# Strassen's scheme for the last group's up projections, and memory visits by 64x64 tiles, in a fused attention and expert kernel

## Chip, cores and metric

One core of a Trainium2 chip runs the whole program in one launch. The metric is the device time in microseconds (us) of an execution, lower is better, given as the median of several runs. Engines are called PE (TensorE's matmuls), PEld (its weight loads), DVE (VectorE), ACT (ScalarE), POOL (GpSimd) and SP (SyncE, which issues the DMAs).

## What is computed

```python
# attention: q, k, v are (4, 8, 576, 64) in float32
a = softmax(causal(q @ k.T / 8)); local = a @ v
q_p = phi(q)                                   # elu + 1
mem = (q_p @ M_prev) / (q_p @ z_prev + 1e-6)   # 64x64 memory of each head
x = sigmoid(beta) * mem + (1 - sigmoid(beta)) * local     # 2304 tokens x 512
# expert: w_gate, w_val 512 x 1536, w_out 1536 x 512
out = (sigmoid(x @ w_gate) * (x @ w_val)) @ w_out
```

The weights arrive as float64 bits and are converted on the chip.

## The kernel before

**Groups.** The 2304 tokens are cut into six groups of 384. Group 0 and group 5 hold the tails of the batches (192 tokens of each of two batches), groups 1 to 4 the first 384 tokens of one batch each. The expert of a group runs while the attention of later groups is done beside it, and the last group's expert has no attention left beside it.

**Expert (`moe`).** Twelve passes, one for each block of 128 of the 1536 inner columns. Every operand is held as a high and a low part in float32r, and a product is three matmuls: high by high, high by low, low by high. A pass has an up part, gate and value projection with 24 matmuls that load a 128x128 block of weights and move 384 tokens (2 projections x 4 blocks of 128 inner features x 3), and a down part of the pass before it (`down`) with 9 matmuls that load 128 tokens and move 512 columns. Between the two stands the gate chain: tanh of the gate's bank on ACT (L895), times the value's bank on DVE (L897), a high copy `gh` on ACT, the rest `gl` on DVE. Each matmul of the program has its own weight load, also where the same block is loaded twice running. The expert's matmuls all have line L313. The up parts take banks 3 and 4 ("gv"), the down parts add up in banks 0 to 2.

**Weights.** In group 0 DVE and ACT convert them (L805 to L816). The gate's high and low parts stay in `wg`; the value's and the output's go to DRAM (`scratch`) and come back by DMA through a ring of three buffers `sv` in the groups that follow.

**Attention.** It goes by pairs of heads: `scores` (`heads`, L561), softmax on DVE and ACT (L623, L635), `turn` (transposes), `values` (L317), `across` (into the group's tokens `xh`, `xl`). The 16 pairs of groups 1 to 4 have two items of scores each. Behind the scores of their first item (256 keys) come the memory visits (`terms`, L518): both heads lie on a half of the array's rows each, three blocks of 128 queries are loaded as 64x128 blocks, and 65 columns move. In the pairs of groups 0 and 5 the visits and the scores ahead of them are by 64x64 blocks already. Float32 matmuls stand twice in the trace for each one in the code.

**Order.** Nothing is issued as the code runs: `Program` collects every instruction with a cost and its dependencies, a list scheduler with priorities (`LEAD`, by part and engine) puts them in an order for each engine, a random search of 800 rounds betters the priorities, and the order is then fixed. An engine works its list in that order.

Of the kernel before, what the change touches and what calls it, by code (L numbers as in the profile page):

```python
# [9 lines left out]
F32 = mybir.dt.float32  # L10
F32R = mybir.dt.float32r
# [10 lines left out]
VC = 66  # L22
# [13 lines left out]

WORLDS = (380.0, 0.85, 0.0), (400.0, 0.85, 0.03), (350.0, 1.0, 0.06)

LEAD = {("attention", "pe"): 150, ("weights", "sp"): 200, ("first", "sp"): 1000, ("second", "sp"): 98}

WAKE = {
    "act": {"act": 0.14, "dve": 0.13, "pe": 0.26, "pool": 0.2, "sp": 0.14},
# [196 lines left out]
def tile_attention_memory_moe(  # L239
# [26 lines left out]
    class Ring:  # L266
# [10 lines left out]
        def take(self):  # L277
            i = self.at % self.n
            self.at += 1
            k = pg.renew((self.name, i))  # L280
            if i not in self.tiles:
                home = self.tags.get(i)
                if home:

                    hosts, ring, at = home
# [4 lines left out]
                    pg.before[(self.name, i)] = set(pg.touched[(ring, at)][1]) | pg.before[(self.name, i)]  # L290
                    pg.closed.add((ring, at))
# [8 lines left out]
    turns = {"att": 0, "gv": 0, "second": 0}  # L300

    def bank(kind):
        ids = {"att": att_banks, "gv": [3, 4], "second": [0, 1]}[kind]
# [7 lines left out]
    def matmul(out, lhsT, rhs, n, r, w, start, stop):  # L311
        pe(0.004 + max(n, 128) / 2250.0,
           lambda: nc.tensor.matmul(out=out, lhsT=lhsT, rhs=rhs, start=start, stop=stop), r, w)  # L313

    def product(out, lhsT, rhs, n, r, w, start, stop):
        pe(0.068 if n <= 100 else 4 * n / 2385.0,
# [8 lines left out]
    def copy(out, in_, n, r, w):  # L325
        act(n, lambda: nc.scalar.copy(out=out, in_=in_), r, w)  # L326
# [76 lines left out]
    kq_r = Ring("kq", [128, 2 * GT], F32R, 4, {i: (in_wt, "wt", i) for i in range(4)})  # L403
    ql_r = Ring("ql", [128, GT], F32R, 2, {i: (in_wr, "wr", 2) for i in range(2)}, init=half)
# [4 lines left out]
    tl_r = Ring("tl", [128, 2 * DM], U16, 2, {i: (turned, "wr", 1) for i in range(2)})  # L409
    xs_r = Ring("xs", [128, 3, 2, D], F32, 2)  # L410
    xm_r = Ring("xm", [128, 3, 2, D], F32, 2)
    rs_r = Ring("rs", [128, 3, 2], F32, 2)
# [96 lines left out]
    def terms(u, sp, js, at):  # L509

        for c in range(3):
            cells = [(0, 128 * c, 0, 128)]
            if u.tail:
                es = (0, 1) if c == 2 else (c, c)
                cells = [(e, e * TL + (128 if c == 2 else m0), m0, m0 + 64) for e, m0 in zip(es, (0, 64))]
            for e, q, m0, m1 in cells:
                for j, r in enumerate(js):
                    nc.tensor.matmul(  # L518
                        out=sp[j][0][m0:m1, at + MC * c:at + MC * c + MC], lhsT=u.ph[r, q:q + m1 - m0],
                        rhs=mem[u.g][e][0][r, u.p, MC * j:MC * j + MC], start=True, stop=True)  # L520
# [44 lines left out]
    def scores(n, x):  # L565
# [11 lines left out]

        def part(i, cells):
            sp = [bank("att") for _ in js]
            more = pair and i == 1 or not u.tail and x == 0  # L580
            work, at = [], 0
            for y, k0, k1 in cells:
                c, q0, W = u.items[x][y]
                if pair:
                    es = [(0, 128, 0, 64), (1, 128, 64, 128)]
                    mk, mk_k = (mask2[:, :k1 - k0], "mask2") if i else (mask[:, :k1 - k0], "mask")
                else:
                    es = [(c if u.tail else 0, q0, 0, 128)]
                    mk, mk_k = mask[:, 512 - W:], "mask"
                work.append((y, es, k0, k1, at, mk, mk_k))  # L590
                at += k1 - k0
            if more:
                u.told = [(sp[j][0][:, at:at + 3 * MC].rearrange("p (c j x) -> p c j x", c=3, j=1),
                           sp[j][1], j, j + 1) for j in range(2)]

            def together():
                for _, es, k0, k1, o, _, _ in work:
                    heads(u, es, sp, js, k0, k1, o)
                if more:
                    terms(u, sp, js, at)  # L600
# [217 lines left out]
    def weights(F):  # L818
# [5 lines left out]
        if g and at < sv_r.n:  # L824
            ready_w[F] = ready_w[F - 2 * at - 1]
            return
        part, pg.part = pg.part, "weights"
        sv_r.at = at if g % 2 == 0 else sv_r.n - 1 - at % sv_r.n
        sv, k = sv_r.take()
        kg = [("wg", f, "h"), ("wg", f, "l")]  # L830
        if g == 0:
# [14 lines left out]
    def rows(g, t):  # L846
# [4 lines left out]
            return [((b + t) * S + GT, 0, 128)]  # L851
        return [((b + e) * S + GT + 128, 64 * e, 64) for e in range(2)]

    def moe(g):
        (xh, _), (xl, _), xk = x_t[g]
        prev = None
# [4 lines left out]
        def down(f, gh, gl, wo):  # L861
# [3 lines left out]
            for t in order:  # L865
# [5 lines left out]
                           f == 0 and i == 0, f == NF - 1 and i == 2)  # L871
                yield

        for f in range(NF):
            cur = ready_w[g * NF + f]
            pz = [bank("second" if g == 0 and f == 1 else "gv") for _ in range(2)]
            turns = [(part, kd) for part in range(2) for kd in range(KD)]
            if f == 0 or g == 0 and f == 1:
# [28 lines left out]
                kept[NF - 1 - f]([gh[1]])  # L907
            if prev:
                yield from down(*prev)
            weights(g * NF + f + 2)  # L910
            prev = (f, gh, gl, cur[2])
        yield from down(*prev)
        for t in order:
            acc, acc_k = accs[t]
            ob, ob_k = (ob_r if g < NG - 1 else at_r).take()
# [110 lines left out]
```

## Time and profile before

| what | value |
|---|---|
| median of 3 runs | 629.06 us (628.87 to 629.29) |
| profiled execution | 629.38 us |
| its span, first to last instruction | 627.5 us |
| PE busy / PEld busy | 610.7 / 535.5 us |
| DVE / ACT busy | 409.8 / 267.5 us |
| mean granted clock of TensorE | 0.995 |

A matmul's row in the timeline gives its start and its duration to the end of its results, so durations overlap; what a matmul costs in a stream is the distance from its start to the next one's, here called its step. An "x12" row is twelve instructions merged. Times in timelines and chains are from the span's start.

### The profile page before, as it was taken

The numbers are of one execution on the slowest core, as the hardware profiler recorded it, in microseconds if no ns is written. First come the engines' busy times: TensorE is split into PE (matmuls) and PEld (weight loads), VectorE is DVE, ScalarE is ACT, GpSimd is POOL, SyncE is SP. The second block draws the span as 40 slices with busy tenths as digits, with TensorE's granted clock in tenths as the row PEclk, the third lists the DMA queues.
The fourth block names the chain that finished last, engine by engine and source line by source line (L and its number), as shares of the span: only waits on it lengthen the run. The fifth ranks groups of instructions, "written<-read, shape, count | busy, mean of one in ns | idle before, by whom it ended". The sixth has DMA issues, their size and how long they took to land.

```text
span 627.5 us, 12396 instructions
## 1 busy us (share of the span) xinstructions
PE 610.7 (97%) x4928; PEld 535.5 (85%) x4928; DVE 409.8 (65%) x1091; ACT 267.5 (43%) x536; POOL 9.5 (2%) x51
## 2 busy tenths in 40 slices
PE   6889999998999999999999999999999999999996
PEld 3559888986898988898988898988898989999995
DVE  4999999998865568756566756678697573121211
ACT  6997667756533324333242434246363221211111
POOL 2000000000000000000000000000000000000000
PEclk9999999999999999999999999999999999999999
DMA  8667878796499699668786467978668994225351
GB/s 303 231 229 240 270 283 276 249 311 225 93 281 297 210 217 254 116 174 216 187 219 209 107 173 211 223 203 229 139 147 219 181 218 146 100 84 191 146 194 57
DMA packets 103130, 126.42 MB, mean 201 GB/s; under 512 B 79648, under 2 KB 81696, under 8 KB 95776
## 3 DMA queue, kind: packets, MB, share of 16 engines
q1 hardware_dynamic: 102928, 125.36, 69.7%
q8 instruction: 39, 0.64, 0.4%
q10 hardware_dynamic: 144, 0.26, 0.1%
q14 instruction: 19, 0.16, 0.1%
HBM read 89.43 MB, written 17.30 MB: 170 GB/s over the span
## 4 chain that ended last, share of the span: by engine, by line
PE 90%; DVE 6%; DMA 1%; ACT 1%; issue 1%; DVEq 0%; ACTq 0%
PE bank L313 72%; PE bank L317 7%; PE bank L561 6%; PE bank L320 2%; PE bank L518 2%; DVE a L623 1%; DMA wr<-in_w_dram 1%; DVE wt L809 1%; DVE wt L812 1%; ACT a L635 1%; DVE sv L336 1%; DMA kp<-in_qk_dram 1%; DVE wt L807 0%; DVE ph L492 0%; ACT wt L805 0%
## 5 line engine op out<-in xcount | busy, mean ns | idle before, releaser
L313 PE MATMUL bank<-xh,wg 128*128 128x384 f32 x576 | 163.4, 341 | 2.2 <-ACT wg L326 2.0
L313 PE MATMUL bank<-xh,sv 128*128 128x384 f32 x576 | 164.1, 341 | 0.3 <-DVE th L897 0.2
L313 PE MATMUL bank<-sv,gh 128*128 128x512 f32 x432 | 136.2, 396 | 0.3 <-ACT gh L326 0.3
L313 PEld LDWEIGHTS bank<-xh,wg 128*128 128x128 f32 x576 | 104.8, 188 | 8.8 <-ACT wg L326 2.8
L313 PEld LDWEIGHTS bank<-xh,sv 128*128 128x128 f32 x576 | 104.8, 188 | 2.8 <-DVE sv L336 0.7
L897 DVE SCALAR_TENSOR_TENSOR th<-th,bank 128x384 f32<-128x384 f32 x72 | 39.7, 551 | 98.0 <-PE bank L313 96.9
L313 PE MATMUL bank<-xl,wg 128*128 128x384 f32 x288 | 97.8, 340 | 0.0
L313 PE MATMUL bank<-xl,sv 128*128 128x384 f32 x288 | 97.6, 339 | 0.0
L313 PEld LDWEIGHTS bank<-sv,gh 128*128 128x128 f32 x432 | 79.5, 188 | 14.2 <-ACT gh L326 0.7
L895 ACT ACTIVATE th<-bank 128x384 f32<-128x384 f32 x72 | 35.3, 490 | 131.0 <-PE bank L313 130.8
L635 ACT ACTIVATE a<-a,st 128x256 f32<-128x256 f32 (+4 forms) x144 | 77.3, 581 | 26.9 <-DVE st L623 26.3
L623 DVE CUSTOM_DVE_ANT_0 a<-bank,mask 128x256 f32<-128x256 f32 (+3 forms) x144 | 64.9, 485 | 36.3 <-PE bank L561 18.3
L313 PE MATMUL bank<-sv,gl 128*128 128x512 f32 x216 | 84.8, 396 | 0.0
L326 ACT CAST gh<-th 128x384 fp32r<-128x384 f32 x72 | 36.9, 513 | 104.7 <-DVE th L897 104.5
L313 PEld LDWEIGHTS bank<-xl,wg 128*128 128x128 f32 x288 | 54.1, 188 | 4.1 <-issue 1.0
L561 PE MATMUL bank<-kp 64*128 64x256 f32 (+4 forms) x352 | 52.5, 452 | 4.0 <-DMA kp<-in_qk_dram 4.0
L653 DVE COPY at<-tl_wr 128x1024 uint16<-128x1024 uint16 (+1 forms) x72 | 46.8, 654 | 12.7 <-DMA tl_wr<-pl_wr 12.5
L313 PEld LDWEIGHTS bank<-xl,sv 128*128 128x128 f32 x288 | 54.1, 188 | 0.5
L336 DVE TENSOR_TENSOR gl<-th,gh 128x384 fp32r<-128x384 f32 x72 | 39.8, 554 | 15.5 <-ACT gh L326 15.2
L313 PEld LDWEIGHTS bank<-sv,gl 128*128 128x128 f32 x216 | 40.5, 188 | 9.4 <-DVE gl L336 0.4
L649 DVE COPY pl_wr<-a 128x1024 uint16<-128x1024 uint16 (+1 forms) x72 | 41.8, 593 | 3.8 <-ACT a L635 3.8
L561 PEld LDWEIGHTS bank<-kp 64*128 64x128 f32 (+1 forms) x352 | 23.1, 169 | 23.8 <-issue 10.5
(66 smaller groups left out, 588.0 us busy)
## 6 DMA issues: line engine op xcount, KB each, us to landing
sv<-w SPq DMA_DIRECT2D x45, 1024.0 KB, 5.4
wr<-in_w_dram SPq DMA_DIRECT2D x36, 512.0 KB, 4.6
kp<-in_qk_dram SPq DMA_DIRECT2D x32, 384.0 KB, 4.1
w<-sv SPq DMA_DIRECT2D x12, 1024.0 KB, 6.6
out_dram<-ob SPq DMA_DIRECT2D x14, 256.0 KB, 2.2
vt<-in_vp_dram SPq DMA_DIRECT2D x8, 330.0 KB, 4.8
vr<-in_vp_dram SPq DMA_DIRECT2D x8, 330.0 KB, 4.1
mb<-in_mz_dram SPq DMA_DIRECT2D x8, 260.0 KB, 3.5
```

Of the source, the lines that this page charges most:

```text
L313: lambda: nc.tensor.matmul(out=out, lhsT=lhsT, rhs=rhs, start=start, stop=stop), r, w)
L317: lambda: nc.tensor.matmul(out=out, lhsT=lhsT, rhs=rhs, start=start, stop=stop), r, w)
L320: pe(0.110, lambda: nc.tensor.transpose(out=out, in_=in_, identity=identity), r, w)
L326: act(n, lambda: nc.scalar.copy(out=out, in_=in_), r, w)
L336: dve(n, lambda: nc.vector.tensor_tensor(out=out, in0=in0, in1=in1, op=op), r, w)
L561: nc.tensor.matmul(out=sp[j][0][m0:m1, at:at + k1 - k0], lhsT=kp[r, u.qa + q:u.qa + q + m1 - m0], rhs=kp[r, u.ka + k0:u.ka + k1], start=Tr ...
L623: dve(m + 60, lambda aj=aj, sj=sj, pj=pj, o=o, m=m, mk=mk, b=b0 + k0: nc.vector.tensor_tensor_reduce(out=aj[:, b:b + m], in0=pj[:, o:o + m ...
L635: act(W + 120, lambda aj=aj, sj=sj, b=b0, W=W: nc.scalar.activation(out=aj[:, b:b + W], in_=aj[:, b:b + W], func=AF.Exp, scale=-1.0, bias= ...
L649: dve(2 * W, lambda: nc.vector.tensor_copy(out=pl.rearrange("p (two w) -> p two w", two=2), in_=src), r, [pk], fast=True)
L653: dve(2 * W, lambda: nc.vector.tensor_copy(out=dst, in_=tl.rearrange("p (two w) -> p two w", two=2)), [lk], [key], fast=True)
L895: act(GT, lambda: nc.scalar.activation(out=th, in_=pg_[:, :GT], func=AF.Tanh, scale=0.5), [pg_k], [th_k])
L897: dve(GT, lambda: nc.vector.scalar_tensor_tensor(out=th, in0=th, scalar=1.0, in1=pv[:, :GT], op0=ALU.add, op1=ALU.mult,), [th_k, pv_k], [t ...
```

## The change

Two things. **First**, `terms` and the scores ahead of it load two blocks of 64x64 for each block of 64x128, in the 16 pairs of groups 1 to 4. **Second**, in the last group gate and value projection of a pass are seen as one product of a 2x2 block matrix of weights (gate and value by halves of the 512 input features) with a 2x2 block matrix of tokens (halves of the features by halves of the 384 tokens), done by seven block products in place of eight (`seven`): each has 2 feature blocks x 3 matmuls that load 128x128 and move 192 tokens, so 42 matmuls of 192 tokens stand for 24 of 384. Its inputs are sums: four of the tokens for the whole group (`token_sums`), four of the weights for each pass (`weight_sums`: eight adds or subtractions of 256 columns on DVE, and four splits into high and low, each a copy on ACT and a subtraction on DVE). For passes over blocks 8, 5, 3 and 1 the weight sums are made in groups 2 and 3 and written to DRAM (`save`); for the other eight in or ahead of the last group. Results are put together on DVE from the banks (five adds of 192 columns, the value's product in two halves). Buffers of the attention are given new tenants, and two more sets of value and output weights are held in the last group. The planner's priority of the sums is lower by 60, and its cost of a block of scores with a visit rises from 0.63 to 0.8 us beside the keys' share.

```diff
+SAVED = (8, 5, 3, 1)
+LEAD = {..., ("sums", "dve"): -60, ("sums", "act"): -60}
...
+        ids = {"att": att_banks, "gv": [3, 4], "second": [0, 1], "last": [3, 4, 5, 6, 7]}[kind]
...
+    un_r = Ring("un", [128, DM], F32R, 16, ...)     # weight sums, in a, vr, vt, kp, mb
+    xv_r, xo_r = ...                                # two more sets of weights, in at
...
     def terms(u, sp, js, at):
         for c in range(3):
-            cells = [(0, 128 * c, 0, 128)]
+            cells = [(0, 128 * c + m0, m0, m0 + 64) for m0 in (0, 64)]
...
                     es = [(c if u.tail else 0, q0, 0, 128)]
+                    if more:
+                        es = [(0, q0, 0, 64), (0, q0 + 64, 64, 128)]
...
-                    pe(4 * at / 2385.0 + (0.63 if more else 0.3), together,
+                    pe(4 * at / 2385.0 + (0.8 if more else 0.3), together,
...
+    def weight_sums(F, raws, made):
...
+        whole(a, g, 0)
+        whole(b, v, 0)
+        over(c, b, a)
+        done(2, c)
+        whole(c, g, 1)
+        over(a, a, c, plus)
+        done(0, a)
+        over(b, a, b)
+        done(1, b)
+        whole(c, v, 1)
+        over(c, c, b)
+        done(3, c)
...
+    def seven(g, F, t):
...
+        x, y, z = (bank("last") for _ in range(3))
+        def times(out, a, b, first):
+            (o, ok), (ah, al, ahk, alk), (bh, bl, bhk, blk) = out, a, b
+            for d in range(2):
+                at = slice(d * 128, d * 128 + 128)
+                for i, (l, lk, r, rk) in enumerate(((ah, ahk, bh, bhk), (ah, ahk, bl, blk), (al, alk, bh, bhk))):
+                    matmul(o[:, :HT], l[:, at], r[:, d], HT, lk + rk, [ok], first and d == 0 and i == 0, d == 1 and i == 2, not first)
...
+        times(x, a11, b11, True)
+        copy(p1, x[0][:, :HT], HT, [x[1]], [p1k])
+        times(y, s2, t2, True)
+        plus(u2, y[0][:, :HT], p1, HT, [y[1], p1k], [u2k])
+        times(z, s1, t1, True)
+        times(x, a12, b21, False)
+        times(y, s3, t3, False)
+        plus(u3, y[0][:, :HT], p1, HT, [y[1], p1k], [u3k])
+        plus(gg[:, HT:], z[0][:, :HT], u3, HT, [z[1], u3k], [gk + (1,)])
+        times(y, a22, t4, False)
+        plus(gg[:, :HT], y[0][:, :HT], p1, HT, [y[1], p1k], [gk + (0,)])
+        times(z, s4, b22, False)
+        plus(vv, z[0][:, :HT], u2, HT, [z[1], u2k], [vk])
+        return gg, [gk + (0,), gk + (1,)], [(x[0][:, :HT], x[1]), (vv, vk)]
...
     def moe(g):
+        fast = g == NG - 1
+        if fast:
+            for F in range(g * NF + 2, g * NF + 5):
+                weights(F)
+            t_sums = token_sums(g)
+            for F in range(g * NF, g * NF + 3):
+                units_of(F)
...
+            if g in (2, 3):
+                now = f if g == 2 else NF - 1 - f
+                if now in (SAVED[1:] if g == 2 else SAVED[:1]):
+                    save(g * NF + f, now)
```

## Rows read from the trace of the kernel before

**Rows 1.** The page: busy time of PE, and its share of the span.

```profile
PE 610.7 (97%) x4928; PEld 535.5 (85%) x4928; DVE 409.8 (65%) x1091; ACT 267.5 (43%) x536; POOL 9.5 (2%) x51
```

**Rows 2.** Windows: length, busy us (instructions) by engine, clock, DMA share, GB/s.

```profile
core 0: us, PE busy (x) PEld busy (x) DVE busy (x) ACT busy (x) POOL busy (x), PEclk, DMA share, GB/s
50.00:166.00 116.00, 113.49 (x945) 98.93 (x941) 108.16 (x280) 75.93 (x151) 1.70 (x10) 1.00 0.74 248
166.00:525.00 359.00, 358.81 (x2906) 319.32 (x2905) 241.33 (x646) 130.92 (x268) 4.15 (x16) 1.00 0.78 199
525.00:551.00 26.00, 26.00 (x138) 24.27 (x136) 5.74 (x11) 5.95 (x12) 0.00 (x0) 1.00 0.35 119
551.00:623.00 72.00, 71.68 (x374) 66.30 (x372) 14.04 (x25) 12.67 (x26) 0.00 (x0) 1.00 0.36 132
```

**Rows 3.** Chain that ended last, in time: start, us, what.

```profile
143.67 0.60 DVE wt L809
...
551.34 71.42 PE bank L313 x372
```

**Rows 4.** Timeline of PE over one pass of the last group.

```profile
555.61 0.63 PE L313 MATMUL bank<-sv,gh 128*128 128x512 f32 x2
...
557.69 0.33 PE L313 MATMUL bank<-xh,wg 128*128 128x384 f32 x1
...
561.91 0.63 PE L313 MATMUL bank<-sv,gh 128*128 128x512 f32 x2
```

**Rows 5.** Timeline of PE and its weight loads behind a pause of 0.38 us.

```profile
551.33 0.19 PEld L313 LDWEIGHTS bank<-xh,wg 128*128 128x128 f32 x1 [0.38 <-ACT th L895]
551.34 0.44 PE L313 MATMUL bank<-xh,wg 128*128 128x384 f32 x1
...
551.44 0.19 PEld L313 LDWEIGHTS bank<-xl,wg 128*128 128x128 f32 x1
551.62 0.34 PE L313 MATMUL bank<-xl,wg 128*128 128x384 f32 x1
```

**Rows 6.** Timeline of PE, a visit by 64x128 blocks (group 1 to 4).

```profile
176.78 0.70 PE L561 MATMUL bank<-kp 64*128 64x256 f32 x4
177.32 0.78 PE L518 MATMUL bank<-mb,ph 64*128 64x65 f32 x12
178.03 0.44 PE L313 MATMUL bank<-xl,sv 128*128 128x384 f32 x1
```

**Rows 7.** Timeline of PE, a visit by 64x64 blocks (group 5).

```profile
452.09 0.66 PE L561 MATMUL bank<-kp 64*64 64x256 f32 x8
452.57 0.53 PE L518 MATMUL bank<-mb,ph 64*64 64x65 f32 x24
453.03 0.44 PE L313 MATMUL bank<-xh,wg 128*128 128x384 f32 x1
```

**Rows 8.** DVE's groups by line and shape: count, busy us, mean ns, idle before.

```profile
L336 DVE TENSOR_TENSOR gl<-th,gh 128x384 fp32r<-128x384 f32 x72 | 39.8, 554 | 15.5 <-ACT gh L326 15.2
L336 DVE TENSOR_TENSOR xm<-bank,rn 128x192 f32<-128x192 f32 x48 | 16.2, 351 | 0.2
L623 DVE CUSTOM_DVE_ANT_0 a<-bank,mask 128x256 f32<-128x256 f32 x32 | 12.4, 421 | 14.2 <-PE bank L518 14.2
```

**Rows 9.** Windows of line L518 alone: columns PE and PEld.

```profile
50.00:143.00 93.00, 4.49 (x72) 4.93 (x72) 1.00 0.81 274
166.00:400.00 234.00, 7.82 (x120) 8.33 (x120) 1.00 0.78 203
```

**Rows 10.** Waits of DVE from 50 to 166 us: us, times, longest.

```profile
DVE a L623 <- PE bank L518: 1.5, 3, 0.7
```

**Rows 11.** Timeline of DVE: the last of group 5's tokens.

```profile
532.13 0.56 DVE L336 TENSOR_TENSOR xl<-xm,xh 128x384 fp32r<-128x384 f32 x1
```

**Rows 12.** Timeline: the last pass's gate chain.

```profile
618.22 0.33 PE L313 MATMUL bank<-xh,sv 128*128 128x384 f32 x1
...
618.66 0.55 DVE L897 SCALAR_TENSOR_TENSOR th<-th,bank 128x384 f32<-128x384 f32 x1 [4.62 <-PE bank L313]
...
619.25 0.51 ACT L326 CAST gh<-th 128x384 fp32r<-128x384 f32 x1 [2.22 <-DVE th L897]
```

More of the change, by code (lines that the diff above doesn't have):

```diff
@@ L37 @@
 WORLDS = (380.0, 0.85, 0.0), (400.0, 0.85, 0.03), (350.0, 1.0, 0.06)
-LEAD = {("attention", "pe"): 150, ("weights", "sp"): 200, ("first", "sp"): 1000, ("second", "sp"): 98}
+SAVED = (8, 5, 3, 1)
+LEAD = {("attention", "pe"): 150, ("weights", "sp"): 200, ("first", "sp"): 1000, ("second", "sp"): 98,
+        ("sums", "dve"): -60, ("sums", "act"): -60}
 WAKE = {
@@ L283, in take @@
                 if home:
-                    hosts, ring, at = home
+                    hosts, ring, at, *since = home
                     if hosts[at] is None:
@@ L289, in take @@
                     self.tiles[i] = hosts[at][:, place:place + self.shape[1]]
-                    pg.before[(self.name, i)] = set(pg.touched[(ring, at)][1]) | pg.before[(self.name, i)]
-                    pg.closed.add((ring, at))
+                    for tenant in ((ring, at), *since):
+                        pg.before[(self.name, i)] = set(pg.touched[tenant][1]) | pg.before[(self.name, i)]
+                        pg.closed.add(tenant)
                 else:
@@ L299, in tile_attention_memory_moe @@
     att_banks = list(range(8))
-    turns = {"att": 0, "gv": 0, "second": 0}
+    turns = {"att": 0, "gv": 0, "second": 0, "last": 0}
     def bank(kind):
-        ids = {"att": att_banks, "gv": [3, 4], "second": [0, 1]}[kind]
+        ids = {"att": att_banks, "gv": [3, 4], "second": [0, 1], "last": [3, 4, 5, 6, 7]}[kind]
         turns[kind] += 1
@@ L309, in pe, with matmul @@
         pg.add("pe", cost, emit, r, w)
-    def matmul(out, lhsT, rhs, n, r, w, start, stop):
-        pe(0.004 + max(n, 128) / 2250.0,
-           lambda: nc.tensor.matmul(out=out, lhsT=lhsT, rhs=rhs, start=start, stop=stop), r, w)
+    def matmul(out, lhsT, rhs, n, r, w, start, stop, more=False):
+        pe(0.004 + max(n, 128) / 2250.0, lambda: nc.tensor.matmul(
+            out=out, lhsT=lhsT, rhs=rhs, start=start, stop=stop, skip_group_check=more), r, w)
     def product(out, lhsT, rhs, n, r, w, start, stop):
@@ L402, in tile_attention_memory_moe @@
     plain, turned = {"wide": 4 * DM, 0: None}, {"wide": 4 * DM, 1: None}
-    kq_r = Ring("kq", [128, 2 * GT], F32R, 4, {i: (in_wt, "wt", i) for i in range(4)})
-    ql_r = Ring("ql", [128, GT], F32R, 2, {i: (in_wr, "wr", 2) for i in range(2)}, init=half)
+    in_um, in_rm = {"wide": DM, **dict.fromkeys(range(4))}, {"wide": 2 * GT, 2: None}
+    um_r = Ring("um", [128, DM], F32R, 4, {i: (in_um, "wt", i) for i in range(4)})
+    rm_r = Ring("rm", [128, 2 * GT], F32, 1, {0: (in_rm, "wr", 2)})
+    kq_r = Ring("kq", [128, 2 * GT], F32R, 4, {i: (in_wt, "wt", i, ("um", i)) for i in range(4)})
+    ql_r = Ring("ql", [128, GT], F32R, 2, {i: (in_wr, "wr", 2, ("rm", 0)) for i in range(2)}, init=half)
     a_r = Ring("a", [128, 640], F32, 6, init=pad)
@@ L826, in weights @@
             return
+        if g == NG - 1 and at % 5 >= sv_r.n:
+            part, pg.part = pg.part, "weights"
+            parts = []
+            for ring, i in ((xv_r, 0), (xo_r, 1)):
+                t, k = ring.take()
+                load(t.bitcast(F32), scratch[f][:, i * 2 * DM:(i + 1) * 2 * DM], 575, [("scratch", f)], [k])
+                parts.append(((t[:, :DM], k), (t[:, DM:], k)))
+            ready_w[F] = [ready_w[f][0], *parts]
+            pg.part = part
+            return
         part, pg.part = pg.part, "weights"
-        sv_r.at = at if g % 2 == 0 else sv_r.n - 1 - at % sv_r.n
+        sv_r.at = at if g % 2 == 0 else sv_r.n - 1 - at % (5 if g == NG - 1 else sv_r.n)
         sv, k = sv_r.take()
@@ L852, in rows, with plus, minus, divide @@
         return [((b + e) * S + GT + 128, 64 * e, 64) for e in range(2)]
+    def plus(out, a, b, n, r, w):
+        tt(nc.vector, ALU.add, out, a, b, n, r, w)
+    def minus(out, a, b, n, r, w):
+        sub(nc.vector, out, a, b, n, r, w)
+    def divide(out, r, n, ks, key):
+        hi, lo = out
+        kh, kl = key + ("h",), key + ("l",)
+        copy(hi, r, n, ks, [kh])
+        minus(lo, r, hi.bitcast(F32), n, ks + [kh], [kl])
+        return kh, kl
+    def weight_sums(F, raws, made):
+        part, pg.part = pg.part, "sums"
+        n = DM // 2
+        (g, v) = ready_w[F][:2]
+        r, k = raws.take()
+        a, b, c = ((r[:, i * n:i * n + n], k + (i,)) for i in range(3))
+        units = [made.take() for _ in range(4)]
+        def whole(out, pair, i):
+            (h, hk), (l, lk) = pair
+            o = slice(i * n, i * n + n)
+            plus(out[0], h[:, o].bitcast(F32), l[:, o].bitcast(F32), n, [hk, lk], [out[1]])
+        def over(out, x, y, f=minus):
+            f(out[0], x[0], y[0], n, [x[1], y[1]], [out[1]])
+        def done(i, x):
+            t, key = units[i]
+            divide((t[:, :n], t[:, n:]), x[0], n, [x[1]], key)
+        whole(a, g, 0)
[10 more added lines that the diff above has]
+        done(3, c)
+        pg.part = part
+        return units
@@ new lines, in units_of @@
+    def units_of(F):
+        f = NF - 1 - F % NF
+        n = DM // 2
+        if f in SAVED:
+            part, pg.part = pg.part, "weights"
+            units = [un_r.take() for _ in range(4)]
+            for i, (t, k) in enumerate(units):
+                load(t.bitcast(F32), saved[f][:, i * DM:(i + 1) * DM], 288, [("saved", f, i)], [k + ("h",), k + ("l",)])
+            pg.part = part
+        else:
+            units = weight_sums(F, rw_r, un_r)
+        summed[F] = [(t[:, :n], t[:, n:], [k + ("h",)], [k + ("l",)]) for t, k in units]
@@ new lines, in save, with token_sums @@
+    def save(F, f):
+        units = weight_sums(F, rm_r, um_r)
+        for i, (t, k) in enumerate(units):
+            load(saved[f][:, i * DM:(i + 1) * DM], t.bitcast(F32), 300, [k + ("h",), k + ("l",)], [("saved", f, i)])
+    def token_sums(g):
+        part, pg.part = pg.part, "sums"
+        (xh, _), (xl, _), xk = x_t[g]
+        made = [tt_r.take() for _ in range(4)]
+        for a in range(2):
+            f, fk = rw_r.take()
+            r, rk = rw_r.take()
+            for i in range(2):
+                d = a + 2 * i
+                plus(f[:, i * GT:i * GT + GT], xh[:, d].bitcast(F32), xl[:, d].bitcast(F32), GT, xk[d], [fk + (i,)])
+            b11, b12, b21, b22 = (f[:, i * HT:i * HT + HT] for i in range(4))
+            t1, t2, t3, t4 = (r[:, i * HT:i * HT + HT] for i in range(4))
+            k1, k2, k3, k4 = (rk + (i,) for i in range(4))
+            fk = [fk + (0,), fk + (1,)]
+            minus(t1, b12, b11, HT, fk[:1], [k1])
+            minus(t2, b22, t1, HT, fk[1:] + [k1], [k2])
+            minus(t3, b22, b12, HT, fk, [k3])
+            minus(t4, b21, t2, HT, fk[1:] + [k2], [k4])
+            for i, x in enumerate((t1, t2, t3, t4)):
+                t, key = made[i]
+                o = a * HT
+                divide((t[:, o:o + HT], t[:, GT + o:GT + o + HT]), x, HT, [rk + (i,)], key + (a,))
+        pg.part = part
+        return [(*(t[:, o:o + GT].rearrange("p (a t) -> p a t", a=2) for o in (0, GT)),
+                 [k + (a, "h") for a in range(2)], [k + (a, "l") for a in range(2)]) for t, k in made]
@@ L854, in moe @@
+    summed = {}
+    saved = {f: dram.tile([128, 4 * DM], F32, name=f"s{f}") for f in SAVED}
     def moe(g):
@@ L872, in down @@
                 yield
+        fast = g == NG - 1
[5 more added lines that the diff above has]
+                units_of(F)
         for f in range(NF):
             cur = ready_w[g * NF + f]
+            if fast:
+                th, th_k = th_r.take()
+                gh, gl = gh_r.take(), gl_r.take()
+                gg, gg_k, vals = yield from seven(g, g * NF + f, t_sums)
+                act(GT, lambda th=th, gg=gg: nc.scalar.activation(
+                    out=th, in_=gg, func=AF.Tanh, scale=0.5), gg_k, [th_k])
+                for i, (v, v_k) in enumerate(vals):
+                    o = slice(i * HT, i * HT + HT)
+                    dve(HT, lambda th=th, v=v, o=o: nc.vector.scalar_tensor_tensor(
+                        out=th[:, o], in0=th[:, o], scalar=1.0, in1=v, op0=ALU.add, op1=ALU.mult,
+                    ), [th_k, v_k], [th_k + (i,)])
+                ks = [th_k, th_k + (0,), th_k + (1,)]
+                copy(gh[0], th, GT, ks, [gh[1]])
+                minus(gl[0], th, gh[0].bitcast(F32), GT, ks + [gh[1]], [gl[1]])
+                if prev:
+                    yield from down(*prev)
+                if 0 < f and f + 4 < NF:
+                    weights(g * NF + f + 4)
+                if f + 3 < NF:
+                    units_of(g * NF + f + 3)
+                prev = (f, gh, gl, cur[2])
+                continue
             pz = [bank("second" if g == 0 and f == 1 else "gv") for _ in range(2)]
@@ L914, in moe @@
             acc, acc_k = accs[t]
-            ob, ob_k = (ob_r if g < NG - 1 else at_r).take()
+            ob, ob_k = (rw_r if g == NG - 1 and t == order[2] else ob_r).take()
             o = ob[:, :DM]
```

39 lines of the change are left out of this document (38 added, 1 removed).

## The prediction

> **What bounds the kernel now.** The page comes first: PE is busy 97% of the span, and its count of matmuls equals that of weight loads [rows 1]. The windows then say where that holds. From 50 to 166 us DVE works 108.2 of 116 us, so in this stretch, where the weights are converted, two engines are near their limit. From 166 us to the end PE has hardly a pause (358.8 of 359, 26.0 of 26, 71.7 of 72), while DVE falls to two thirds and then to a fifth; the granted clock is 1.00, so these rows are all at the 2.4 GHz level [rows 2]. The chain in time agrees: it goes over into DVE's conversion at 143.67 us, and its last piece is one run of 372 PE matmuls [rows 3]. A PE microsecond saved or added behind 166 us therefore counts in full; one before 143 us counts only as far as DVE follows.
>
> A busy PE says nothing of its pace, so the steps come from the timeline. In a pass of the last group the 9 matmuls of the down part take 557.69 - 555.61 = 2.08 us, 0.231 each, and the 24 of the up part 4.22 us [rows 4]. The chain's last run holds 264 up matmuls (eleven passes) and 108 down: 71.42 less 108 x 0.231 = 46.5 us, less 0.17 by which the last one's record is longer than its step, gives 0.1753 us for a matmul of 384 tokens [rows 3].
>
> **The seven products, PE's part.** They remove 12 x 24 = 288 matmuls of 384 tokens, 288 x 0.1753 = 50.5 us, and add 12 x 42 = 504 of 192 tokens. No row has a 128x128 load followed by 192 columns, so its step is bounded. As a stream limited by columns, the two steps give (0.231 - 0.1753)/128 = 0.00044 us a column, so 0.1753 - 192 x 0.00044 = 0.091; at the very least half of 0.1753, 0.088. As a stream limited by weight loads, the load behind a pause tells: PE had stood still, the first load went out at 551.33, the second at 551.44, the second matmul began only at 551.62 [rows 5]. With an empty array nothing but the first load keeps the second back, so a 128x128 load takes about 0.109. Beside 384 tokens that is hidden in 0.175; beside 192 (0.091 at most) it isn't. Loads by themselves show the same pace: twelve loads of 64x128 with 65 columns each take 0.71 us from the first to the next kind, on two row halves, so six in a row of about 0.11, although with 64x64 blocks the same columns pass in 0.46 us for twenty-four, six in a row on four blocks, 0.08 at most [rows 6, 7]. So I take 0.109: 504 x 0.109 = 54.9 us, **+4.4 us**. Bounds: 0.107 to 0.112, +3.4 to +6.0, and, were the load hidden after all, 44.4 to 45.9, that is -6.1 to -4.6.
>
> The Trainium skill ("TensorE: Matmul & The Clock Gate", section "Back-to-back issue gap") gives an isolated matmul of N columns N/2.4 + 2.5 ns when warm, 82.5 ns for 192. By that alone the products would take 504 x 0.0825 = 41.6 us, 8.9 us less than before. The same page, section "LDWEIGHTS (loading the stationary operand)", gives columns/1.2, thus 107 ns for a load of 128, and by that 53.9 us, 3.4 more than before. The trace's 0.109 behind the pause is with the second.
>
> **Their chain on DVE and ACT.** In a pass the order on PE has two places that wait for DVE: the sixth product writes onto bank y, which the add before it must have read, and the down part needs `gh`. From rows: a result is read 0.44 - 0.175 = 0.27 us after its matmul's step, a 192-wide add from a bank takes 0.35, ACT follows DVE after 0.04 and copies 384 in 0.51 [rows 8, 12]; about 0.05 more wakes PE. First wait: 0.27 + 0.35 + 0.05 = 0.67. Second, from the last product: 0.27, three DVE operations of 0.35 (the value's add, two half products), 0.04, 0.51, 0.05 and a load of 0.11, 2.03 us. Cover: the down part of the pass before, 2.08 us, and in all passes but the last two products of the next pass (1.3 us; five banks allow x and y). 2.08 + 1.3 is more than 2.70, so eleven passes hide it. In the last pass 0.6 us is bare, where before 18 down matmuls covered the chain; I take **+0.7** (0.3 to 2, as the fixed order fits or not). Waits in the order that I can't place: **+0.3** (0 to 2.5).
>
> **The sums.** Each pass that makes its own takes 12 DVE operations of 256 columns; the row for 256 has 0.42, between 0.351 and 0.554 for 192 and 384 [rows 8]: 5.0 us, eight times, 40 us. Putting together takes five adds, two half products and the split, 7 x 0.351 + 0.554 = 3.0, twelve times, 36 us. The token sums are 4 of 384 and 16 of 192, 7.8 us. Together 84 us with every duration counted whole. DVE has nothing of the attention left after 532.7 us, when the last tokens are split [rows 11], was busy 5.7 of 26 us up to 551 and 14.0 of 72 after [rows 2], and the first up part of the group starts some 24 x 0.175 = 4.2 us before 551.3, at about 547. Token sums and one pass, 12.8 us, fit in the 14 us ahead of it; from there DVE has 71 us of work in 80 us of PE (12 x (42 x 0.109 + 2.08)). So I cost the sums at nothing: what hides them is PE's own slower pass. Without that cover a pass that makes sums takes 8.0 us on DVE against 6.7 on PE.
>
> The four saved passes cost 48 operations more in groups 2 and 3, where DVE works 241 of 359 us, and 4 MB each way. In the last group's windows DMA moves 132 GB/s at a share of 0.36 [rows 2], so 1 MB costs some 2.7 us of all engines: 11 us over two groups at a share of 0.78, 11 in the last. Nothing for both (up to 0.5).
>
> **The memory visits.** From the first matmul of the scores to the next kind it is 178.03 - 176.78 = 1.25 us with 64x128 blocks, and 453.03 - 452.09 = 0.94 with 64x64 [rows 6, 7], with the same 256 keys and 65 columns: 0.31 us, and group 5's blocks have exactly the new form. Of the 16 visits 10 lie behind 166 us (120 instructions of 12 each), where PE is the bound: **-3.1 us**. Six lie before 143 us [rows 9], where DVE's conversion ends last. DVE waited for visits there 1.5 us in all, in three places [rows 10]; three times 0.31 is 0.9 at the most by that way, and I take **-0.5** (0 to -1.8, if all six count). The dearer cost of a visit in the planner moves its order, not a duration.
>
> **Sum.** +4.4 + 0.7 + 0.3 - 3.1 - 0.5 = +1.8, with a new order in the first 166 us good for 1.2 either way, since the search starts afresh. The profiled execution took 629.38, 1.9 beyond its span and 0.3 over the median; on the median of 629.06 it makes 630.9 us.
>
> **Rivals.** *Loads hidden, faster.* If a load takes less of a step than the one row says, 0.091 holds: -4.6 + 0.7 + 0.3 - 3.6 = -7.2, 621.9 us (620.4 at 0.088). For it: the down parts show no cost of loads; against it: 0.109 with an array at rest. It decides from a load shorter than 0.091. Chance 0.08. The gap rule of the Trainium skill quoted above would be this rival, further down still.
>
> *All visits pay, no bare wait.* +4.4 + 0.3 - 4.9 = -0.2, 628.9 us. It needs DVE to follow in the conversion; against it its 93% there. Chance 0.2.
>
> *Visits bring nothing.* Were four 64x64 blocks with the same keys no quicker than two, or were what they free lost to other waits, +5.4, 634.5 us. Against it rows 7, though with two batches' keys there. Chance 0.1.
>
> *DVE sets the last group's pace.* If the sums come late, because their priority is lower and gates go first, the five own passes behind the first three each lose up to 8.0 - 6.7 = 1.3 us: +1.8 + 5 x 1.3 x 0.7 or so, 635 us. For it 71 of 80 us; against it, durations overlap: a 512-wide operation counts 0.60 in the chain [rows 3]. Chance 0.1.
>
> **Numbers.** The forecast has the rest, 0.52; its own range is 629 to 633. Only the first rival, half of the last, and the edges are left out by 627.5 to 635.5. A change under 0.2% (1.26 us) can hardly be told from none: same is 627.8 to 630.3. Slower: the forecast 0.41, visits without gain 0.1, DVE 0.1, together 0.61. Same: 0.10 of the forecast and 0.14 of the second rival, 0.24. Faster: 0.08 of the first rival, 0.06 of the second, 0.01 of the forecast, 0.15.
>
> **What would show it.** In the profile after: a step of 0.109 between products' starts (0.09 would break the main term); a pass of 6.6 to 6.8 us in the last group; visits of 0.94 us in groups 1 to 4 too; DVE's conversion ending near 165 us as before; PE's pauses behind 525 us under 1.5 us in all. The prediction is wrong if the step is short, if the first 166 us change by more than 1.5 us, or if PE waits for sums.

## The result, and the profile after

The changed kernel takes 634.2 us (median of 7 runs, 632.5 to 637.0) against 628.5 of the kernel before in the same rounds: 1.0093 times as long, 95% interval 1.0069 to 1.0116, **5.7 us slower**. The profiled execution took 634.2 us, its span 632.4. The direction held and so did the range of 627.5 to 635.5 us; the forecast's own inner range of 629 to 633 didn't, and its +1.8 us was too small by 3.9.

The page of the changed kernel, first part:

```profile
PE 612.6 (97%) x5400; PEld 535.0 (85%) x5400; DVE 482.7 (76%) x1327; ACT 291.6 (46%) x604; POOL 9.5 (2%) x51
```

PE has 472 matmuls more (216 by the products, 256 by the visits' smaller blocks) and only 1.9 us more busy time than in [rows 1], since the shorter visits take back most of what the products add; DVE has 73 us more. So most of the 5.7 us is not busy time. Its windows, cut as in [rows 2] with the first 50 us added (length, busy us by engine, clock, DMA share, GB/s):

```profile
0.00:50.00 50.00, 40.88 (x582) 27.80 (x584) 40.65 (x133) 41.93 (x82) 3.69 (x25) 0.97 0.77 263
50.00:166.00 116.00, 112.87 (x1047) 97.17 (x1043) 109.20 (x282) 75.40 (x151) 1.10 (x8) 1.00 0.76 246
166.00:525.00 359.00, 356.98 (x3068) 315.65 (x3067) 259.17 (x705) 139.07 (x288) 4.71 (x18) 1.00 0.84 218
525.00:551.00 26.00, 25.78 (x154) 23.71 (x153) 19.66 (x54) 10.39 (x26) 0.00 (x0) 1.00 0.49 137
551.00:632.00 81.00, 76.12 (x563) 70.65 (x561) 54.02 (x157) 24.79 (x57) 0.00 (x0) 1.00 0.43 140
```

PE's last matmul ends at 627.5 us, so most of the gap in the last row is the way of the output. From 166 to 525 us PE now stands still 2.0 us, where it stood 0.2 [rows 2]: a stretch in which the change only adds the saved sums and shortens the visits.

The timeline of PE in the changed kernel, a visit (one of the ten behind 166 us), and then products of the last group:

```profile
175.37 0.66 PE L586 MATMUL bank<-kp 64*64 64x256 f32 x8
175.85 0.53 PE L543 MATMUL bank<-mb,ph 64*64 64x65 f32 x24
176.31 0.44 PE L316 MATMUL bank<-xh,sv 128*128 128x384 f32 x1
...
605.13 1.28 PE L316 MATMUL bank<-tt_wt,un_a 128*128 128x192 f32 x10
606.25 0.27 PE L316 MATMUL bank<-xh,xv_at 128*128 128x192 f32 x1
```

The visit takes 176.31 - 175.37 = 0.94 us, as by 64x64 blocks before [rows 7], not 1.25 [rows 6]. Ten products take 1.12 us, a step of 0.112, not the 0.088 to 0.091 that columns alone would give. Three passes of the last group, from the down part that starts at 600.92 us to the one at 621.15, take 6.74 us each, as forecast (6.6 to 6.8).

### The profile page after: what moved, and what is told of

The parts are those of the page before. It is cut to its first block, busy times and chain, and to the rows that moved or that the text cites. A ratio compares the mean times of both kernels' runs of the same rounds, so it can differ in the third digit from the quotient of the medians.

```text
span 632.4 us, 13747 instructions
## 1 busy us (share of the span) xinstructions
PE 612.6 (97%) x5400; PEld 535.0 (85%) x5400; DVE 482.7 (76%) x1327; ACT 291.6 (46%) x604; POOL 9.5 (2%) x51
## 4 chain that ended last, share of the span: by engine, by line
PE 76%; DVE 11%; ACT 6%; DMA 5%; issue 2%; ACTq 0%; DVEq 0%
PE bank L316 62%; PE bank L321 6%; PE bank L586 5%; DMA xs<-xm 2%; ACT a L662 2%; PE bank L324 2%; DMA s<-um_wt 1%; DVE wt L836 1%; ACT at L330 1%; DVE a L650 1%; PE bank L543 1%; DVE rw_wr L340 1%; DVE gl L340 1%; DVE rm_wr L340 1%; DMA tl_wr<-pl_wr 1%
## 5 line engine op out<-in xcount | busy, mean ns | idle before, releaser
L316 PE MATMUL bank<-xh,sv 128*128 128x384 f32 (+1 forms) x544 | 150.0, 333 | 0.3 <-ACT th L1106 0.2
L316 PE MATMUL bank<-xh,wg 128*128 128x384 f32 x480 | 136.9, 341 | 1.9 <-DVE wg L340 0.9
L662 ACT ACTIVATE a<-a,st 128x256 f32<-128x256 f32 (+3 forms) x144 | 77.7, 583 | 36.8 <-DVE st L650 36.2
L316 PEld LDWEIGHTS bank<-xh,wg 128*128 128x128 f32 x480 | 87.4, 188 | 7.7 <-DVE wg L340 1.9
L316 PE MATMUL bank<-xl,sv 128*128 128x384 f32 (+1 forms) x272 | 90.4, 332 | 0.0
L650 DVE CUSTOM_DVE_ANT_0 a<-bank,mask 128x512 f32<-128x512 f32 (+2 forms) x144 | 65.0, 485 | 28.8 <-PE bank L586 18.9
L316 PE MATMUL bank<-xl,wg 128*128 128x384 f32 x240 | 81.8, 341 | 0.0
L586 PE MATMUL bank<-kp 64*64 64x256 f32 (+4 forms) x416 | 50.7, 436 | 4.1 <-DMA kp<-in_qk_dram 4.0
L316 PEld LDWEIGHTS bank<-xl,wg 128*128 128x128 f32 x240 | 45.1, 188 | 3.8 <-issue 1.0
L586 PEld LDWEIGHTS bank<-kp 64*64 64x64 f32 (+1 forms) x416 | 21.4, 155 | 24.9 <-issue 11.3
```

Of the source, the lines that this page charges most:

```text
L316: pe(0.004 + max(n, 128) / 2250.0, lambda: nc.tensor.matmul(out=out, lhsT=lhsT, rhs=rhs, start=start, stop=stop, skip_group_check=more), r, w)
L586: nc.tensor.matmul(out=sp[j][0][m0:m1, at:at + k1 - k0], lhsT=kp[r, u.qa + q:u.qa + q + m1 - m0], rhs=kp[r, u.ka + k0:u.ka + k1], start=Tr ...
L662: act(W + 120, lambda aj=aj, sj=sj, b=b0, W=W: nc.scalar.activation(out=aj[:, b:b + W], in_=aj[:, b:b + W], func=AF.Exp, scale=-1.0, bias= ...
```

## Experiments

All are compared with the kernel before on the same chip. There were several chips, on which that kernel's median was 628.4 to 629.4 us (experiments 1 to 4 ran on one, 5 to 7 on another, 8 on a third, 9 and 10 on a fourth), so a difference of medians between experiments of two chips can be off by up to 1 us. Where nothing is said, the kernel computes the same result.

**1. Visits alone.** The kernel before, with this:

```diff
-            cells = [(0, 128 * c, 0, 128)]
+            cells = [(0, 128 * c + m0, m0, m0 + 64) for m0 in (0, 64)]
+                    if more:
+                        es = [(0, q0, 0, 64), (0, q0 + 64, 64, 128)]
-                    pe(4 * at / 2385.0 + (0.63 if more else 0.3), together,
+                    pe(4 * at / 2385.0 + (0.8 if more else 0.3), together,
```

> The kernel before with the 64x64 visits and the planner's dearer visit, without Strassen's products. My theory: each of 16 visits takes 0.94 in place of 1.25 us, the ten behind 166 us count in full (-3.1), the six ahead of 143 us count too, since the changed kernel was 2.6 us ahead after twelve passes: -3.1 to -4.9, so 623.7 to 625.5 us. Rival 1, that DVE's conversion swallows the six: -3.1 and no more. Rival 2, that what is saved is lost again to waits in a new order whatever else is done: 627 to 629.

Measured: 621.6 us (621.4 to 622.1), ratio 0.9883 (0.9863 to 0.9902), 6.75 us faster than before: more than any of the three expected, so something besides the visits' 4.9 helps. It is also the fastest version here, with experiment 6.

**2. Strassen alone.** The changed kernel with visits by 64x128 blocks:

```diff
-            cells = [(0, 128 * c + m0, m0, m0 + 64) for m0 in (0, 64)]
+            cells = [(0, 128 * c, 0, 128)]
-                    if more:
-                        es = [(0, q0, 0, 64), (0, q0 + 64, 64, 128)]
```

> The changed kernel with visits by 64x128 blocks as before; all of Strassen's part stays. If products cost +5.4, the bare end +0.6 and the saves' late buffers +1.6 to 2, it is 7.5 to 8.5 us over the kernel before, 636 to 637 us. Rival: the two parts disturb each other (the visits' new order makes the waits), then it is 5.4 + 0.6, about 634.5 us.

Measured: 638.2 us (636.7 to 641.6), ratio 1.0164 (1.0127 to 1.0201), 9.9 us slower. That is over both ranges: Strassen's part costs more than its known terms. Against the changed kernel the visits are worth 4.0 us here, near the 4.5 of experiments 7 and 1, so nothing shows that the two parts disturb each other.

**3. Saves earlier.** The changed kernel, with all four in group 2:

```diff
-                if now in (SAVED[1:] if g == 2 else SAVED[:1]):
+                if now in (SAVED if g == 2 else ()):
```

> The changed kernel, but all four saves are made in group 2, none in group 3, where the fourth one's buffers and its DMA held up the next user of the same buffers. If that chain makes the pause of 1.5 us near 396 us, it goes: 632 to 632.7 us, and the runs lie closer together than 632.5 to 637. Rival: the pause is a flaw of this order as any order has some, and turns up elsewhere: 634 us, with the same spread.

Measured: 631.5 us (629.5 to 634.0), ratio 1.0046 (1.0028 to 1.0064). The time fell by 2.7 us. The windows from 385 to 400 us, of the changed kernel and then of this one (columns as above), show that the pause near 396 us is gone: PE is busy 13.50 us of 15 in the one and all 15 in the other.

```profile
385.00:400.00 15.00, 13.50 (x69) 12.00 (x69) 13.12 (x33) 10.80 (x23) 0.12 (x1) 1.00 0.89 242
```

```profile
385.00:400.00 15.00, 15.00 (x81) 13.67 (x82) 10.97 (x28) 8.46 (x18) 0.00 (x0) 1.00 0.70 213
```

But the runs lie no closer together, and another pause has come, in this kernel's timeline of PE and then of DVE (in brackets the idle time ahead of the instruction, and what ended it):

```profile
240.42 0.45 PE L316 MATMUL bank<-xh,sv 128*128 128x384 f32 x1 [1.57 <-DVE th L1108]
```

```profile
238.33 0.43 DVE L340 TENSOR_TENSOR rm_wr<-sv 128x256 f32<-128x256 f32 x1 [2.11 <-DMA sv<-w]
...
239.82 0.54 DVE L1108 SCALAR_TENSOR_TENSOR th<-th,bank 128x384 f32<-128x384 f32 x1
```

An operation of a save, `rm_wr<-sv`, waits on DVE for the DMA of the weights that it reads, and the gate chain's `th`, for which PE waits, stands behind it in DVE's list. From 166 to 525 us PE stands still 359 - 356.2 = 2.8 us, more than the 2.0 of the changed kernel. So the pause near 396 us hung on the fourth save's place, but the 2.7 us were not won by its going: ahead of 166 us PE is busy 156.2 us here and 153.8 in the changed kernel, by another order, and behind it the saves wait elsewhere.

**4. Half the columns.** The changed kernel, each product moving 96 tokens; half of the last group's up projections are left out:

```diff
-                    matmul(o[:, :HT], l[:, at], r[:, d], HT, ...)
+                    matmul(o[:, :HT // 2], l[:, at], r[:, d, :HT // 2], HT, ...)
```

> The changed kernel, each of the 504 products moving 96 tokens in place of 192 (half of the tokens' up projections are left out); the order and all else stay. If loads of 128x128 set the step, it stays at 0.11 us and the time at 634 us within 1. Rival, that columns set the step: 96 x 0.00044 = 0.042 us less each, 504 times: 21 us faster, 613 us.

Measured: 640.2 us (median of 637.1, 637.9, 642.5 and 693.0 us, at mean granted clocks of 0.990, 0.990, 0.984 and 0.906), ratio 1.0161 (1.0113 to 1.0208) without the last. Not faster at all, though half the columns are gone. Its timeline of PE, at the granted clock of 1.00 and then in a stretch where it was lower:

```profile
600.69 0.28 PE L316 MATMUL bank<-xh,un_mb 128*128 128x96 f32 x1
...
601.36 0.46 PE L316 MATMUL bank<-sv,gh 128*128 128x512 f32 x1
```

```profile
554.41 1.48 PE L316 MATMUL bank<-tt_wt,un_a 128*128 128x96 f32 x6
555.69 0.63 PE L316 MATMUL bank<-tt_wt,un_vt 128*128 128x96 f32 x2
```

Six products take 601.36 - 600.69 = 0.67 us, 0.112 each, the same as with 192 tokens: the weight loads set the step. In the other stretch six take 1.28 us, 0.213 each. The windows of this kernel show why:

```profile
545.00:551.00 6.00, 6.00 (x52) 5.81 (x50) 5.57 (x17) 4.07 (x12) 0.00 (x0) 1.00 0.36 134
551.00:562.00 11.00, 11.00 (x48) 10.19 (x47) 6.71 (x20) 2.97 (x8) 0.00 (x0) 0.53 0.00 0
562.00:619.00 57.00, 57.00 (x436) 53.82 (x434) 41.64 (x121) 18.19 (x43) 0.00 (x0) 1.00 0.55 185
619.00:627.00 8.00, 8.00 (x36) 7.13 (x36) 2.52 (x7) 1.03 (x2) 0.00 (x0) 0.57 0.00 0
```

The granted clock is 0.53 there and 0.57 in a second stretch, the 1.2 GHz level for most of both, and loads take twice as long. By an estimate from these rows that costs 11 x 0.47 + 8 x 0.43 = 8.6 us; the profiled execution's 642.5 less 8.6 is 633.9, the expected 634. So the lower clock is why the whole got slower, and it didn't fall in the last group of the changed kernel.

**5. Saves alone.** The visits-only kernel with the saves of the changed one, which nobody reads; the last group as before:

```diff
-        fast = g == NG - 1
+        fast = False
```

(and the last group's loads and output buffers as before). 

> The visits-only kernel (621.6 us) with the four saves of the changed kernel in groups 2 and 3 added, whose result nobody reads; the last group is as before, without Strassen. My theory now: the saves are not free, since they fill DVE's queue and hold buffers that the last attention group's keys take next; the changed kernel lost 2.7 us against the visits-only kernel between its passes 36 and 42. So 623.5 to 625 us, with a PE pause of over 1 us near 390 us. Rival, the price that I predicted: 621.6 to 622.1 us, and the loss belongs to the order as a whole.

Measured: 625.9 us (625.3 to 626.6), ratio 0.9959 (0.9944 to 0.9974). With the saves it takes 4.3 us more than the visits-only kernel's 621.6 (4.8 by the two ratios), more than either expectation. Its windows and those of the visits-only kernel, from 166 to 525 us, the one below the other:

```profile
166.00:525.00 359.00, 357.09 (x3071) 316.17 (x3070) 257.30 (x690) 136.58 (x281) 4.54 (x18) 1.00 0.83 211
```

```profile
166.00:525.00 359.00, 358.89 (x3084) 318.64 (x3083) 240.66 (x643) 130.34 (x267) 2.29 (x16) 1.00 0.77 201
```

1.9 us of PE pauses against 0.1 in the stretch where the saves are made, 1.2 of them between 385 and 400 us (PE busy 13.77 of 15), where over 1 was expected. The chain that ended last has, in this kernel (start, us, what):

```profile
377.58 7.74 DMA s<-um_wt
...
385.40 0.78 ACT kq_wt L330
...
392.63 7.83 DMA sv<-w
...
400.59 1.11 PE bank L316 x5
```

The keys `kq` are written when the save's DMA has landed, and the weights `sv` that PE then waits for are loaded late behind them. Ahead of 163 us no operation of a save stands, and yet PE is busy 2.0 us less in the first 50 us (40.24 against 42.27, at a granted clock of 0.97 against 1.00) and 0.4 less from 50 to 166 (112.35 against 112.77). That part goes with the order that the search found and with PE's clock; that the saves themselves cause it is not shown.

**6. Scores by 64x64 too.** The visits-only kernel with `if not u.tail:` in place of `if more:`.

> The visits-only kernel with the second item's scores of the 16 pairs by 64x64 blocks as well. A block of scores without a visit takes 1.07 us by 64x128 blocks for 512 columns, 0.21 over the 0.85 of its columns at four passes and full clock; by 64x64 it takes 0.70 for 320, 0.17 over. So 0.05 us each, 16 times, 0.8 us: 620.8 us. Rival: the entry of a block is set by the drain, not by its loads: 621.6 us.

Measured: 621.7 us (621.3 to 622.5), ratio 0.9893 (0.9878 to 0.9908). No difference to experiment 1 that these runs can tell: the expected 0.8 us didn't come, the rival's 621.6 fits.

**7. The planner's cost alone.** The kernel before with 0.8 for 0.63, nothing else:

> The kernel before with nothing but the planner's cost of a visit raised from 0.63 to 0.8 us, so only the order of instructions differs. The visits-only kernel gained 6.75 us where sixteen times 0.306 is 4.9; if the better order by the truer cost is the rest, this kernel is 1 to 2 us faster than before, 626.5 to 627.5 us. Rival: the rest is chance of the search, or PE's clock kept up in the first 50 us by shorter visits: 628.4 within 0.6.

Measured: 626.1 us (625.7 to 626.7), ratio 0.9962 (0.9949 to 0.9974). The order alone is worth 2.2 us, and the visits, from here to experiment 1, 4.5 (5.0 by the two ratios). The windows of the kernel before and of this one place the order's gain:

```profile
0.00:50.00 50.00, 40.76 (x579) 26.67 (x581) 40.52 (x133) 41.70 (x81) 3.69 (x25) 0.97 0.72 257
```

```profile
0.00:50.00 50.00, 42.23 (x612) 28.17 (x613) 40.59 (x134) 42.72 (x84) 3.68 (x25) 1.00 0.76 258
```

Up to 166 us PE is busy 155.2 us here and 154.3 before, 1.0 more, and the clock in the first 50 us is 1.00 for 0.97, by an estimate another 0.03 x 41 = 1.2 us: the 2.2 us, all ahead of 166 us, and the clock rose with visits as long as before.

**8. No saves.** The changed kernel, all twelve passes making their own sums:

```diff
-SAVED = (8, 5, 3, 1)
+SAVED = ()
...
-    kq_r = Ring("kq", [128, 2 * GT], F32R, 4, {i: (in_wt, "wt", i, ("um", i)) for i in range(4)})
+    kq_r = Ring("kq", [128, 2 * GT], F32R, 4, {i: (in_wt, "wt", i) for i in range(4)})
```

(and likewise `ql`: the keys' buffers no longer wait for the saves' `um` and `rm`). 

> The changed kernel with no saved sums: all twelve passes of the last group make their own, visits by 64x64 stay. Against the visits-only kernel (621.6 us) only Strassen's last group is left. If PE's loads set that group's pace and DVE's operations cost their steps (0.33 for 256 columns, 12 to a pass, 2.3 us to put together: 6.3 us a pass against PE's 6.7), it is 621.6 + 6.4 = 628 us, 6 us faster than the changed kernel. Rival, DVE at whole durations (8.0 us a pass): the nine passes behind the first three lose 1.3 us each, 640 us, with PE waiting for DVE between passes.

Measured: 629.1 us (628.6 to 629.8), ratio 0.9999 (0.9989 to 1.0008): 5.1 us faster than the changed kernel by the medians, 5.9 by the ratios. Its windows:

```profile
0.00:50.00 50.00, 41.48 (x612) 28.24 (x613) 40.63 (x135) 42.69 (x84) 3.70 (x25) 1.00 0.74 261
166.00:525.00 359.00, 358.88 (x3084) 318.44 (x3083) 246.20 (x657) 132.41 (x272) 4.20 (x16) 1.00 0.80 207
```

The chain that ended last in its profile (start, us, what), from 540 us:

```profile
539.99 82.13 PE bank L316 x614
622.12 0.02 issue
622.14 0.60 ACT rw_wr L1134
```

PE never waits for a sum, though DVE makes half again as many of them there. Its timeline of DVE shows what such an operation costs in a stream:

```profile
573.57 0.55 DVE L340 TENSOR_TENSOR gl<-th,gh 128x384 fp32r<-128x384 f32 x1
574.04 0.42 DVE L340 TENSOR_TENSOR un_vt<-rw_wr,un_vt 128x256 fp32r<-128x256 f32 x1
574.38 0.42 DVE L340 TENSOR_TENSOR rw_wr<-rw_wr 128x256 f32<-128x256 f32 x1
574.71 0.35 DVE L340 TENSOR_TENSOR u_xm<-bank,p_ph 128x192 f32<-128x192 f32 x1
574.98 0.42 DVE L340 TENSOR_TENSOR rw_wr<-sv 128x256 f32<-128x256 f32 x1
```

0.34 and 0.33 from start to start where the record says 0.42, 0.27 where it says 0.35, 0.47 where it says 0.55: by an estimate from these a pass with sums takes 12 x 0.33 + 7 x 0.27 + 0.47 = 6.3 us, less than PE's 6.7. Against experiment 1, Strassen's last group alone costs 7.5 us by the medians and 6.7 by the profiled spans (627.0 and 620.3).

**9 and 10. Another seed.** Experiment 1 and the changed kernel with `random.Random(2)`, so another order of the same instructions.

> The visits-only kernel with another seed of the planner's random search, so another order of the same instructions. It sizes the chance in the search: if orders found by it lie within 0.5 us of each other, 621.1 to 622.2 us; if the first 166 us are a lottery, as the 2.2 us that a changed cost alone gave suggest, anywhere from 620.5 to 625 us.

> The changed kernel with that other seed. My theory, that the saves cost some 2.5 us behind pass 36 through the buffers that they hold for the last attention group's keys, and the rest early by chance: 2 to 3 us lost again between passes 36 and 42 against its visits-only twin, and 631 to 635 us in all. Rival, that the whole 5 us over the kernel without saves is chance of one order: 629 to 630 us.

Measured: 625.5 us (623.3 to 626.6), ratio 0.9949 (0.9933 to 0.9964), and 634.0 us (633.1 to 635.0), ratio 1.0088 (1.0061 to 1.0115). The visits-only kernel lost 3.9 us by another order (its profiled execution, at 623.3 us, only 1.7), so the search is a lottery of up to that size; the changed kernel came out as before. With this seed the whole of Strassen costs 8.4 us, with the first 12.6. PE's pause from 166 to 525 us stays with the saves: 359 - 357.5 = 1.5 us in the changed kernel of this seed, 359 - 358.6 = 0.4 in the visits-only one. A kernel without saves was not run with this seed.

## Why the prediction held in direction and range, and where it failed

**Luck.** Without the saves the changed kernel takes 0.9999 of the time before (experiment 8): what the prediction worked out as +1.8 came out as no change that these runs can tell. The loss that makes "slower" true comes with the term that it put at nothing, the saves. So, as far as experiment 8 shows, the direction held by luck, not by the sum's mechanism. Two rivals lie near 634.2 us in number alone: visits without gain (634.5) is out by experiment 1, DVE setting the pace (635) by experiment 8.

**The products.** The step of 0.109 was forecast from one load behind a pause [rows 5], and came out as 0.112; 504 x 0.003 adds 1.5 us to the term. Experiment 4 shows that loads set it. The Trainium skill ("TensorE: Matmul & The Clock Gate", section "LDWEIGHTS (loading the stationary operand)") gives columns/1.2 ns, by estimate 107 ns for 128 columns, near the trace's 112. The same page's gap for a matmul alone (section "Back-to-back issue gap"), by estimate 82.5 ns at 192 columns, is not the step of this stream. For the last group as a whole +5.4 was forecast, for products, bare end and odd waits; 6.7 to 7.5 was measured (experiment 8 against 1), without any bare end. Of it the step explains 504 x 0.112 - 50.5 = 5.9 us; the rest isn't traced, and some of it may be order, since up to 166 us, where the last group has no part, PE is busy 0.9 us less in experiment 8 than in 1 (154.2 against 155.0). The rival with hidden loads is out.

**The bare end.** Forecast 0.7 (0.6 by the working). In the changed kernel's chain (start, us, what):

```profile
623.58 0.02 issue
623.60 0.36 DVE vv_xs L340
623.96 0.56 DVE th L1073 x2
...
624.60 0.52 ACT gh L330
...
625.16 2.38 PE bank L316 x9
```

It goes through the very operations of the working, 1.58 us from the end of PE's last product (623.58) to the down part that needs `gh` (625.16). A part of another down part fills most of it; what stays bare is in the timeline there:

```profile
625.16 0.97 PE L316 MATMUL bank<-sv,gh 128*128 128x512 f32 x3 [0.41 <-ACT gh L330]
```

0.4 for the forecast 0.7. Experiment 8's chain has no such piece, so another order hides it.

**The visits.** The price of 0.31 each was right, and that only about twelve of the 16 would count (3.6 / 0.306) was wrong: 4.5 us from experiment 7 to experiment 1 are nearly fifteen, the 5.0 by the ratios all sixteen. That DVE is 93% busy up to 166 us [rows 2] didn't keep PE's time from counting. The forecast was -3.6.

**The sums.** Costed at nothing, with 71 us of DVE work in 80 of PE. Right, and safer than reckoned, since durations overlap (experiment 8). The rival in which DVE sets the pace is out.

**The saves: the step that failed.** "Nothing for both (up to 0.5)" rested on DVE's and the DMA's shares of busy time. With them the changed kernel takes 5.1 us more than without (experiment 8), and the visits-only kernel 4.3 more (experiment 5 against 1); some 2 us of either are shown to be the saves' own. From 166 to 525 us neither was full (DVE busy 259 of 359 us, DMA's share 0.84); between 385 and 400 both nearly were (13.1 of 15, 0.89). In the changed kernel's chain (start, us, what):

```profile
376.81 0.36 DVE um_wt L340 x2
377.17 7.10 DMA s<-um_wt
...
384.35 0.70 ACT kq_wt L330
...
388.81 0.69 DVE kq_wt L340
...
390.43 0.70 DVE pl_wr L676
...
391.16 4.51 DMA tl_wr<-pl_wr
...
397.53 0.50 PE bank L316
```

The sums of the fourth save lie in `um`, in the memory of `wt`, whose next tenant is `kq`, the split keys of the last attention group. The save's DMA must have read them before ACT may write `kq`. It takes 7.1 us, and behind it everything is late: the keys, the scores' transpose, its DMA, DVE's queue. The timeline there has the end of it:

```profile
397.53 0.50 PE L316 MATMUL bank<-kq_wt 128*128 128x512 f32 x1 [1.50 <-DVE st L650]
```

The prediction costed the transfer as a share of bandwidth and never asked who takes over its buffer, which the change's line for `kq_r` names (experiment 8 takes it out). Experiment 5 and the changed kernel with the second seed, in other orders, have the same piece, with 7.7 and 6.9 us for the save's DMA. Between 385 and 400 us PE is busy 13.3 to 13.8 of 15 us in all five kernels that make the fourth save in group 3 (the changed kernel, experiments 2, 4, 5 and 10), and all 15 in the seven others. Moved to group 2 the saves wait elsewhere (experiment 3). Of the 5.1 us some 2 are such pauses from 166 to 525 us: PE stands still there for 1.5 to 2.8 us in every kernel with saves and for at most 0.4 in those without. Some 0.4 is the bare end. Of the rest a part lies in the first 50 us, where PE is busy 40.88 us at a granted clock of 0.97, and in experiment 8 41.48 us at 1.00: 0.6 us of pauses, and about 0.03 x 41 = 1.2 of clock. No save stands there, and the kernel before, without any, shows 40.76 us at 0.97 too (experiment 7). So how much of this the saves cause and how much the search's order, which they change as well, stays open: experiments 7 and 9 move 2 to 4 us by order alone.

**The order.** "The dearer cost of a visit in the planner moves its order, not a duration", and 1.2 us either way for a new order. Experiment 7 shows -2.2 for the cost, experiment 9 +3.9 for a seed; the bound was too narrow. By the prediction's own sign of being wrong, a change of more than 1.5 us in the first 166 us, the order of experiment 7 alone (2.2 us, all there) is one.

**The sum.** -2.2 for the order by the new cost, -4.5 for the visits, +7.5 for the last group, +5.1 with the saves: +5.9, measured +5.7. These are the steps from one kernel's median to the next, from the kernel before to the changed one, so that they add up shows nothing of their causes. Forecast were 0, -3.6, +5.4 and 0. The errors are -2.2, -0.9, +2.1 and +5.1: the first three about cancel, which is luck, and the step to the kernel with saves, some 2 us of it shown to be theirs and the rest open, is more than the whole miss of 3.9.

## What to carry to other kernels

Before splitting matmuls into fewer columns, look for the weight load that the longer ones hide: here a load of 128x128 fills 0.11 us, so an eighth less arithmetic in matmuls half as wide cost about 7 us, while loads in smaller blocks (the visits: twenty-four of 64x64 in 0.46 us for twelve of 64x128 in 0.71) gave 4.5. Work put into an engine's idle share isn't free by that share alone: ask which buffer it holds, who is next in it, and how long its transfer takes. And where an order is searched at random, compare parts of a change with the same order or with several, since an order by itself moved this kernel by up to 4 us.

## What the runs showed of the hardware that was not expected

In experiment 4, with 96 columns behind each load, PE was busy without a pause, yet the granted clock fell to about half twice in the last group (0.53 over the 11 us from 551 on, where it had been 1.00, and 0.57 over the 8 us from 619 on), and loads slowed with it, 0.213 for 0.112; with 192 columns, in the changed kernel, it stayed at 1.00. All four executions of that kernel have a lower mean clock (0.906 to 0.990) than the changed kernel's seven (0.995 to 1.0). The narrower matmuls, and the values that come of them, are the only change between the two kernels; why the clock fell is not shown.
